# Two blocks of scores share one mask product, and GpSimd lays out q, in an attention kernel that feeds a mixture of experts

## The chip, the core and the metric

The kernel runs on one core of a Trainium2 chip. The metric is the device time of one execution in microseconds. Before the change the median of three runs is 191.55 us (190.66 to 191.68). One execution was recorded by the hardware profiler; all durations of single instructions come from it.

## The reference

Sliding-window causal attention over 8 batches, 8 heads, 576 positions and a head size of 64, followed by a soft mixture of experts with 8 experts of 4 slots each. Cut to what matters:

```python
scores = scale * np.matmul(q, k.transpose(0, 1, 3, 2))
mask = (rel >= 0) & (rel < 64)               # rel = query position - key position
scores = np.where(mask, scores, -1000000000.0)
scores = scores - np.max(scores, axis=-1, keepdims=True)
attn = np.exp(scores)
attn = attn / (np.sum(attn, axis=-1, keepdims=True) + 1e-09)
x = np.matmul(attn, v)                       # then heads side by side: 4608 x 512
logits = x @ phi                             # 512 x 32
d = softmax of logits over the 4608 tokens   # d.T @ x gives the 32 slots
slot_out[e] = np.maximum(slot_input[e] @ w1[e], 0.0) @ w2[e]      # 512 -> 1024 -> 512
out = (softmax of logits over the 32 slots) @ slot_out
```

All inputs and the output are fp32 in HBM; the kernel computes in fp16 with fp32 accumulation, and the loads of GpSimd's queue convert on the way.

## The kernel before

**Units.** Two heads of one batch make a pair: 32 pairs, numbered p, four to a batch. The 576 positions of a pair are nine blocks of 64 queries, and the window makes each block see 128 keys. One group of loads is two pairs, so there are 16 groups of k, of q and of v.

**q and k.** Rows of q and k arrive with 96 partitions and are turned by TensorE (`st_transpose`, twelve products) into the PSUM banks `a_q` and `a_k`. `st_copy_k` copies k to `kTs` in one 128x576 instruction. `st_copy_q` copies q to `qbs` in two instructions of 64 partitions, one per head: `qbs` holds for each block the two heads beside each other, each with zeros in the other head's partitions, so that one product of 128 columns gives both heads' scores. The zeros are written once (`zero_q`).

**Maxima and scores.** The scores are made twice. First with queries in the partitions: `st_max` lays down the window's mask (two products of 512 columns) and adds eight blocks in `a_m`; `st_max_read` (L356) takes the eight maxima into `ms`; the ninth block has a place of its own (`st_max8`, `st_max8_read`, L366). `st_shift` (L369, L370) turns the nine columns of maxima into nine rows of `rts`. Then `st_scores` makes the scores with keys in the partitions (L375) and adds to each block one more product (L378): `lh` carries the mask in its upper 64 rows and, for block i, a row of minus ones that picks row i of `rts`, so mask and maximum are taken off together. ScalarE exponentiates (`st_exp` L384, `st_exp8` L397) and `st_av` (L408) multiplies by v; a column of ones in v gives the sum. `st_norm` (L417, L418) normalises into `x_b`. `fr_transpose` and its copy turn `x_b` for the logits; `fr_logits`, `fr_exp`, `fr_slots` and `fr_acc` keep a running softmax over tokens, once per batch of four pairs.

**Order.** The order of the instructions of every engine is written out by hand (`manual_schedule`). The loop `for n in range(-1, NP - 1)` handles several pairs at once: in iteration n it turns k of pair n+1 and q of pair n, makes the maxima of pair n-1 (they read q and k of n-1), the shift and the scores of pair n-2, and the value products, normalisation and turn of pair n-4. The first four iterations (`early`) have another order. `kv` marks the iterations in which VectorE copies k (L327) instead of ScalarE (L330): n = 2, and then every fourth.

**GpSimd's queue.** `loads(n)` stands at the head of iteration n. It issues a weight where `WSLOTS` has one (one every 3.2 iterations, 12 in all with the last two), for odd n a load of k, for even n `shift_v`, then a load of v and one of q. `shift_v` (L183, L185) moves v by half a chunk between partitions with two copies, and so waits until that v has landed. `loads` and the softmax's `cb_sub` are all that GpSimd does in the loop. A 1 MB weight (fp16) is one load; v, k and q are 288 KB each. v has two buffers, k and q four.

**After the loop** the last pairs are finished in an order of their own, the last weights are loaded in pieces into buffers that have come free (`load_last1`, `load_half`), the running softmax is closed, and the experts are multiplied (`first`, `second`, `second_last`); the half columns 0 to 255 of the experts' output are done before the other half. `give` makes the output in pieces and SyncE's queue writes them (L905).

Of the kernel before, what the change touches and what calls it, by code (L numbers as in the profile page):

```python
# [18 lines left out]
def kernel(  # L19
# [141 lines left out]
    pqk = ctx.enter_context(tc.tile_pool(name="pqk", bufs=1))  # L161
    pvv = ctx.enter_context(tc.tile_pool(name="pvv", bufs=1))
    pw = ctx.enter_context(tc.tile_pool(name="pw", bufs=2))
    pxb = ctx.enter_context(tc.tile_pool(name="pxb", bufs=2))
    pxt = ctx.enter_context(tc.tile_pool(name="pxt", bufs=1))

# [9 lines left out]
    def shift_v(g):  # L176
        b, gq = divmod(g, 2)
        v1, v2 = v1s[b % 2], v2s[b % 2]
        c0, c1 = NVC * gq, NVC * gq + NVC

        w1, w2 = [t[:, :, :].rearrange("p c x -> p (c x)").bitcast(mybir.dt.int32)
                  .rearrange("p (c x) -> p c x", c=NCH)[:, :, 0:Dh // 2] for t in (v1, v2)]
        nc.gpsimd.tensor_copy(out=w2[64:128, c0:c1, :], in_=w1[0:64, c0:c1, :])  # L183
        c0 = max(c0, 1)
        nc.gpsimd.tensor_copy(out=w2[0:64, c0:c1, :], in_=w1[64:128, c0 - 1:c1 - 1, :])  # L185
# [5 lines left out]
    def warm_up(n):  # L191
        for i in range(n):
# [11 lines left out]

    db = const.tile([128, 12], FP16, name="db")
    nc.vector.tensor_scalar(out=db[64:128, 0:NB], in0=ident_h[64:128, 64:64 + NB], scalar1=-1.0, scalar2=None,
                            op0=ALU.mult)
    nc.vector.tensor_scalar(out=db[64:128, 10:11], in0=ident_h[64:128, 64 + NB:65 + NB], scalar1=NEG, scalar2=None,  # L210
                            op0=ALU.mult)
    nc.vector.tensor_copy(out=db[64:128, 11:12], in_=ident_h[64:128, 64 + NB:65 + NB])
    lh = const.tile([128, NB, 128], FP16, name="lh")
    nc.scalar.copy(out=lh[64:128], in_=db[64:128, 0:NB].unsqueeze(2).broadcast_to([64, NB, 128]))

    NK, NQ = 4, 3
    kTs = [pqk.tile([128, 64 + S], FP16, name=f"kT{i}") for i in range(NK)]
# [11 lines left out]

    no_token()  # L230
    round_rows("ks", 0, nc.scalar.copy)
    nc.vector.tensor_copy(out=lh[0:64], in_=wb[:, :].unsqueeze(1).broadcast_to([64, NB, 128]))
# [4 lines left out]
    nc.vector.memset(wm[:, 0, 0:64], NEG)  # L237
    round_rows("ks", 1, nc.vector.tensor_copy)
    NR = 2
    rts = [const.tile([128, 128], FP16, name=f"rt{i}") for i in range(NR)]  # L240

    def make_rt(rt):
        nc.vector.tensor_copy(out=rt[64:128, :], in_=db[64:128, 11:12].broadcast_to([64, 128]))
        nc.vector.tensor_copy(out=rt[0:64, 0:64], in_=ident_h[0:64, 0:64])
        nc.vector.tensor_copy(out=rt[0:64, 64:128], in_=ident_h[0:64, 0:64])


    ms = [const.tile([128, 128], FP16, name=f"m{i}") for i in range(2)]
# [12 lines left out]
    ssf = const.tile([128, 4, 32], FP32, name="ssf")  # L261
    quarter = const.tile([128, 4], FP32, name="quarter")
    emask = const.tile([128, 2], FP32, name="emask")

    def late_constants(n):
        if n == 0:
            nc.vector.memset(ms[0], 0.0)
            zero_q(1)
        elif n == 1:
            nc.vector.tensor_tensor(out=lh[64:128, 0, 0:64], in0=lh[64:128, 0, 0:64],  # L270
                                    in1=db[64:128, 10:11].broadcast_to([64, 64]), op=ALU.add)
            make_rt(rts[0])
            nc.vector.memset(ms[1], 0.0)
            zero_q(2)
        elif n == 2:
            make_rt(rts[1])
        elif n == 3:
            ones_v(0)
        elif n == 4:
            ones_v(1)  # L280
        elif n == 5:
            nc.vector.tensor_copy(out=phi_sb, in_=phi_f)
            nc.vector.memset(quarter, 0.0)
            for d_ in ds:
                nc.vector.memset(d_[:, 192:256], 0.0)
            nc.vector.memset(nmax[1], 1.0e30)
            nc.vector.memset(stat, 0.0)
        elif n == 7:
            for t in range(4):
                nc.vector.tensor_copy(out=ss[32 * t:32 * t + 32],  # L290
                                      in_=ident_h[32 * t:32 * t + 32, 32 * t:32 * t + 32]
                                      .unsqueeze(1).broadcast_to([32, 4, 32]))
                nc.vector.memset(quarter[32 * t:32 * t + 32, t:t + 1], 1.0)
        elif n == 15:
            nc.vector.tensor_copy(out=ssf, in_=ss)
# [26 lines left out]
    def turned(tq):  # L322
        return tq[:, 0:S].rearrange("p (r g) -> p g r", r=RQ)

    def st_copy_k(p, on_vector=False):
# [3 lines left out]
        else:  # L329
            nc.scalar.activation(kTs[p % NK][:, 64:64 + S], turned(a_kh), AF.Copy, scale=QKS)  # L330

    def st_copy_q(p, both=False):
        for hf in range(2):
            h = slice(64 * hf, 64 * hf + 64)
            if hf and both:
                nc.vector.tensor_scalar(out=qbs[p % NQ][h, :, hf, :], in0=turned(a_qh)[h], scalar1=QKS, scalar2=None,  # L336
                                        op0=ALU.mult)
            else:
                nc.scalar.activation(qbs[p % NQ][h, :, hf, :], turned(a_qh)[h], AF.Copy, scale=QKS)  # L339
# [13 lines left out]
                             start=False, stop=True, skip_group_check=True)  # L353

    def st_max_read(p):
        nc.vector.reduce_max(ms[p % 2][:, 64:72].rearrange("p (l c) -> p l c", l=2),  # L356
                             a_m[:, :, :].rearrange("p l (c x) -> p l c x", x=128), axis=AXX)

    m8 = a_v[:, 0, 384:512]

# [2 lines left out]
        nc.tensor.matmul(m8, qblock(p, 8), kwindow(p, 8), start=False, stop=True, skip_group_check=True)  # L363

    def st_max8_read(p, m8=m8):
        nc.vector.reduce_max(ms[p % 2][:, 72:73], m8, axis=AXX)  # L366

    def st_shift(p, t_=a_v[:, 1, 384:512]):
        nc.tensor.matmul(t_, ms[p % 2][:, :], ident_h[:, :], start=True, stop=True, skip_group_check=True)  # L369
        nc.vector.tensor_copy(out=rts[p % NR][64:64 + NB, :], in_=t_[64:64 + NB, :])  # L370

    def st_scores(p, blocks, at):
        rt = rts[p % NR]
        for i in blocks:
            nc.tensor.matmul(at(i), kwindow(p, i), qblock(p, i), start=(i % 4 == 0), stop=False,  # L375
                             skip_group_check=True)
        for i in blocks:
            nc.tensor.matmul(at(i), lh[:, i, :], rt[:, :], start=False, stop=True, skip_group_check=True)  # L378

    def st_score(p):  # L380
        st_scores(p, range(8), lambda i: a_s[:, i // 4, 128 * (i % 4):128 * (i % 4) + 128])
# [111 lines left out]

    def cb_exp(b):
        ec = pw.tile([128, 6, 32], FP16, name="ec", tag="ec") if b < B - 1 else \
            lh[:, 6:8, :].rearrange("p i x -> p (i x)")[:, 0:192].rearrange("p (i s) -> p i s", s=32)
        nc.scalar.activation(ec[:, :, :], lgs.pop(b)[:, :, :], AF.Exp)
        cbs[b] = ec

# [42 lines left out]
    def loads(n):  # L542
        if n in WSLOTS:
            load_w(WSLOTS[n])
        i, odd = divmod(n, 2)
        if odd:
            if 0 <= i < NG - 4:
                load_k(i + 4)
        elif i > 0:
            shift_v(i - 1)  # L550
            if i + 1 < NG:
                load_v(i + 1)
            if i + 3 < NG:
# [97 lines left out]
    def make_ss4():  # L651
        nc.gpsimd.memset(ss4, 0.0)
        for t in range(4):
            r = slice(32 * t, 32 * t + 32)
            nc.gpsimd.tensor_copy(out=ss4[r, t, :], in_=ss[r, :, :].rearrange("p t s -> p (t s)"))
# [34 lines left out]
    for d in range(2):  # L690
        load_half(d)
    st_score8(p - 3)
# [71 lines left out]
    ssf_ = ssf[:, :, :].rearrange("p t s -> p (t s)")  # L764
# [205 lines left out]
```

## Time and profile before

| what | value |
|---|---|
| median of three runs | 191.55 us (190.66 to 191.68) |
| the profiled execution | 190.24 us, span 188.2 us |
| TensorE busy (matmul) | 160.0 us, 85% |
| VectorE busy | 142.9 us, 76% |
| ScalarE busy | 145.0 us, 77% |
| GpSimd busy | 83.0 us, 44% |
| granted TensorE clock | 0.978 of full speed on average, full until the last two slices |
| read from HBM, written | 61.93 MB, 9.44 MB |
| q copies (L339) | 63, 645 ns each |
| k copies on ScalarE (L330), on VectorE (L327) | 24 of 655 ns, 8 of 746 ns |
| shift copy (L370) | 30, 289 ns each |
| v's loads, issue to landing | 13.3 us median, 8.8 to 19.1 |

How to read it: a line such as `L370 DVE CAST rt<-a_v` is the instruction of line 370 on VectorE (DVE) that writes `rt` and reads `a_v`. PE is TensorE's matmul, PEld its weight load, ACT is ScalarE, POOL GpSimd. Square brackets in a timeline give the idle time of the engine before the instruction and what ended it. The DMA row gives the busy share of the 16 DMA engines in forty slices of the span; a share over 1 in a table of stretches means that packets overlap within an engine.

### The profile page before, as it was taken

The numbers are of one execution on the slowest core, as the hardware profiler recorded it, in microseconds if no ns is written. First come the engines' busy times: TensorE is split into PE (matmuls) and PEld (weight loads), VectorE is DVE, ScalarE is ACT, GpSimd is POOL, SyncE is SP. The second block draws the span as 40 slices with busy tenths as digits, with TensorE's granted clock in tenths as the row PEclk, the third lists the DMA queues.
The fourth block names the chain that finished last, engine by engine and source line by source line (L and its number), as shares of the span: only waits on it lengthen the run. The fifth ranks groups of instructions, "written<-read, shape, count | busy, mean of one in ns | idle before, by whom it ended". The sixth has DMA issues, their size and how long they took to land.

```text
span 188.2 us, 7073 instructions
## 1 busy us (share of the span) xinstructions
PE 160.0 (85%) x3039; PEld 120.5 (64%) x3039; DVE 142.9 (76%) x354; ACT 145.0 (77%) x267; POOL 83.0 (44%) x123
## 2 busy tenths in 40 slices
PE   5777999999999999999999999999899899878400
PEld 1466778877777677777777787777785357543100
DVE  6797786897888789788888878897887734689700
ACT  6677879989889899889898898989478455589500
POOL 7955726171682453862953706707653170000000
PEclk9999999999999999999999999999999999999965
DMA  6999999999999999999999999999999999999996
GB/s 160 223 184 185 228 172 226 175 222 180 185 223 180 213 191 185 201 206 181 209 193 191 211 187 190 203 202 192 216 211 216 205 196 193 247 340 392 417 417 264
DMA packets 62302, 41.47 MB, mean 220 GB/s; under 512 B 38848, under 2 KB 58304, under 8 KB 61376
## 3 DMA queue, kind: packets, MB, share of 16 engines
q0 software_dynamic: 56560, 30.35, 116.7%
q1 hardware_dynamic: 5712, 10.68, 16.0%
q8 instruction: 23, 0.38, 0.7%
q14 instruction: 7, 0.06, 0.1%
HBM read 61.93 MB, written 9.44 MB: 379 GB/s over the span
## 4 chain that ended last, share of the span: by engine, by line
PE 45%; DVE 34%; ACT 6%; DMA 5%; issue 4%; DVEq 0%; SPq 0%; ACTq 0%
DVE m L356 10%; PE a_m L349 5%; DVE x_b L418 5%; PE a_m L352 5%; PE a_v L408 4%; PE a_s L375 4%; PE a_s L378 4%; PE a_q L319 3%; DMA out_dram<-w 3%; PE a_k L432 3%; DVE kT L327 3%; DVE rt L370 2%; DVE acc L529 2%; DMA w<-in_q_dram 2%; PE ha L819 2%
## 5 line engine op out<-in xcount | busy, mean ns | idle before, releaser
L339 ACT ACTIVATE qb<-a_q 64x576 f16<-64x576 f16 x63 | 40.6, 645 | 6.1 <-PE a_q L319 4.9
L356 DVE TENSOR_REDUCE m<-a_m 128x8 f16<-128x1024 f32 x32 | 39.1, 1223 | 1.0
L384 ACT ACTIVATE pt<-a_s 128x1024 f16<-128x1024 f32 x32 | 32.8, 1023 | 6.8 <-PE a_s L378 5.6
L183 POOL COPY v<-v 64x576 int32<-64x576 int32 x16 | 10.6, 661 | 41.1 <-DMA v<-in_v_dram 41.0
L418 DVE TENSOR_TENSOR x_b<-a_v,rc 128x640 f16<-128x640 f32 x31 | 25.6, 824 | 1.1
L352 PEld LDWEIGHTS <-qb 128*128 128x128 f16 x256 | 16.9, 98 | 7.6 <-DVE qb L336 0.3
L349 PE MATMUL a_m<-wm,ident_h 128*128 128x512 f16 x64 | 19.3, 384 | 1.4 <-DVE m L356 1.4
L378 PEld LDWEIGHTS <-lh 128*128 128x128 f16 x288 | 18.7, 98 | 2.0 <-issue 1.7
L173 POOL DMA_DIRECT2D v<-in_v_dram x16 | 19.7, 1234 | 0.0
L375 PEld LDWEIGHTS <-kT 128*128 128x128 f16 x288 | 18.6, 98 | 1.6 <-issue 1.4
L436 ACT COPY xt<-a_k 128x576 f16<-128x576 f16 x28 | 17.9, 639 | 2.2 <-PE a_k L432 0.9
L375 PE MATMUL a_s<-qb,kT 128*128 128x128 f16 x256 | 19.5, 219 | 0.0
L378 PE MATMUL a_s<-rt,lh 128*128 128x128 f16 x256 | 19.5, 219 | 0.0
L352 PE MATMUL a_m<-kT,qb 128*128 128x128 f16 x256 | 19.5, 219 | 0.0
L408 PE MATMUL a_v<-v,pt 128*64 128x65 f16 x558 | 15.6, 196 | 2.4 <-DVE m L366 1.1
L79 POOL DMA_DIRECT2D ks<-in_k_dram x15 | 10.5, 697 | 16.0 <-PE a_s L378 3.8
L370 DVE CAST rt<-a_v 9x128 f16<-9x128 f32 x30 | 8.7, 289 | 10.8 <-PE a_v L369 10.5
L408 PEld LDWEIGHTS <-pt 128*64 128x64 f16 x576 | 13.5, 110 | 4.7 <-DVE m L366 1.8
L330 ACT ACTIVATE kT<-a_k 128x576 f16<-128x576 f16 x24 | 15.7, 655 | 0.8 <-PE a_k L319 0.8
L319 PE MATMUL a_q<-ident_h,qs 96*64 96x96 f16 x384 | 14.8, 206 | 1.2 <-DVE a_q L228 1.1
L319 PE MATMUL a_k<-ident_h,ks 96*64 96x96 f16 x384 | 14.4, 212 | 1.0 <-DVE ks L110 0.8
L901 DVE TENSOR_SCALAR w<-cp,rcs 128x256 f32<-128x256 f32 (+1 forms) x24 | 13.4, 610 | 2.3 <-PE cp L896 1.9
(183 smaller groups left out, 327.8 us busy)
## 6 DMA issues: line engine op xcount, KB each, us to landing
w<-in_moe_w_dram POOLq DMA_DIRECT2D x13, 1024.0 KB, 18.0
out_dram<-w SPq DMA_DIRECT2D x8, 768.0 KB, 6.8
v<-in_v_dram POOLq DMA_DIRECT2D x16, 288.0 KB, 13.3
ks<-in_k_dram POOLq DMA_DIRECT2D x15, 288.0 KB, 15.4
qs<-in_q_dram POOLq DMA_DIRECT2D x15, 288.0 KB, 13.5
out_dram<-w SPq DMA_DIRECT2D x3, 384.0 KB, 4.0
w1h<-in_moe_w_dram POOLq DMA_DIRECT2D x4, 256.0 KB, 16.7
w<-in_moe_w_dram POOLq DMA_DIRECT2D x4, 256.0 KB, 15.3
```

Of the source, the lines that this page charges most:

```text
L173: nc.gpsimd.dma_start(out=v1s[b % 2][:, c, 0:Dh], in_=v[b].rearrange("h s d -> (h s) d").rearrange("(c p) d -> p c d", p=128)[:, c, :])
L319: nc.tensor.transpose(tq[64 * hf:64 * hf + 64, RP * r:RP * r + RP], src[0:RP, h + hf, Dh * r:Dh * r + Dh], ident_h[0:RP, 0:RP])
L339: nc.scalar.activation(qbs[p % NQ][h, :, hf, :], turned(a_qh)[h], AF.Copy, scale=QKS)
L349: nc.tensor.matmul(a_m[:, j, :], ident_h[:, :], wm[:, j:j + 4, :].rearrange("p c x -> p (c x)"), start=True, stop=False, skip_group_check= ...
L352: nc.tensor.matmul(a_m[:, i // 4, 128 * (i % 4):128 * (i % 4) + 128], qblock(p, i), kwindow(p, i), start=False, stop=True, skip_group_chec ...
L356: nc.vector.reduce_max(ms[p % 2][:, 64:72].rearrange("p (l c) -> p l c", l=2), a_m[:, :, :].rearrange("p l (c x) -> p l c x", x=128), axis ...
L375: nc.tensor.matmul(at(i), kwindow(p, i), qblock(p, i), start=(i % 4 == 0), stop=False, skip_group_check=True)
L378: nc.tensor.matmul(at(i), lh[:, i, :], rt[:, :], start=False, stop=True, skip_group_check=True)
L384: nc.scalar.activation(st_pt(p)[:, 0:8, :].rearrange("p i x -> p (i x)"), a_s[:, :, :], AF.Exp, scale=XS)
L408: nc.tensor.matmul(a_v[r0:r0 + 64, hf, 65 * (i // 2):65 * (i // 2) + 65], pt[:, i, 64 * hf:64 * hf + 64], rhs, start=True, stop=True, skip ...
L418: nc.vector.tensor_tensor(out=xbs[b][:, :, 128 * hp:128 * hp + 128].rearrange("p c (l d) -> p l c d", l=2), in0=avv[:, :, :, 0:64], in1=rc ...
L436: nc.scalar.copy(out=xts[b][:, hp, :], in_=th[:, 0:S])
```

## The change

- `lh` has five entries instead of nine. An entry now picks a row for each of two neighbouring blocks, and one product of 256 columns takes mask and maxima off both; the ninth block keeps a product of 128 columns. `rts` is 256 wide. The maxima of even blocks lie in columns 64 to 68 of `ms`, those of odd blocks in columns 96 to 99; the shift's copy becomes a multiplication by `kind`, which zeroes the rows of the other kind in each half.
- From pair 4 to pair 30 q leaves PSUM in one 128x576 copy of ScalarE into `qp` (one buffer), and GpSimd copies its two halves from there into `qbs`, as int32. The first four pairs and the last keep `st_copy_q`.
- k is copied by ScalarE in every iteration but n = 2.
- `loads(n + 1)` stands behind the q copies of iteration n (from n = 3). Weights are issued every 3.6 iterations, nine instead of ten before the last two slots, and one more after the loop; the last `shift_v` moves behind it.
- The fp32 copy `ssf` is made by GpSimd after the loop, in `qp`'s buffer, instead of by VectorE in iteration 15.

```diff
+    NJ = NB // 2 + 1
     db = const.tile([128, 12], FP16, name="db")
-    nc.vector.tensor_scalar(out=db[64:128, 0:NB], in0=ident_h[64:128, 64:64 + NB], scalar1=-1.0, scalar2=None,
+    nc.vector.tensor_scalar(out=db[64:128, 0:NJ], in0=ident_h[64:128, 64:64 + NJ], scalar1=-1.0, scalar2=None,
                             op0=ALU.mult)
+    nc.vector.tensor_tensor(out=db[64:128, 0:NJ], in0=db[64:128, 0:NJ], in1=ident_h[64:128, 96:96 + NJ],
+                            op=ALU.subtract)
...
-    lh = const.tile([128, NB, 128], FP16, name="lh")
+    lh = const.tile([128, NJ, 128], FP16, name="lh")
...
+    kind = const.tile([128, 2, 128], FP16, name="kind")
+    def make_kind():
+        for e in range(2):
+            r = slice(64 + 32 * e, 96 + 32 * e)
+            nc.vector.memset(kind[r, e, :], 1.0)
+            nc.vector.memset(kind[r, 1 - e, :], 0.0)
...
+    def st_copy_q_whole(p):
+        qp = pqp.tile([128, S], FP16, name="qp", tag="qp")
+        nc.scalar.activation(qp, turned(a_qh), AF.Copy, scale=QKS)
+        for hf in range(2):
+            h = slice(64 * hf, 64 * hf + 64)
+            nc.gpsimd.tensor_copy(out=qbs[p % NQ][:, :, :, :].rearrange("p i l x -> p (i l x)").bitcast(mybir.dt.int32)
+                                  .rearrange("p (i l x) -> p i l x", i=NB, l=2)[h, :, hf, :],
+                                  in_=qp[h, :].bitcast(mybir.dt.int32).rearrange("p (i x) -> p i x", i=NB))
...
-        nc.vector.reduce_max(ms[p % 2][:, 64:72].rearrange("p (l c) -> p l c", l=2),
-                             a_m[:, :, :].rearrange("p l (c x) -> p l c x", x=128), axis=AXX)
+        m = ms[p % 2][:, 64:128].rearrange("p (e x) -> p e x", e=2)[:, :, 0:4]
+        nc.vector.reduce_max(m.rearrange("p e j -> p j e"),
+                             a_m[:, :, :].rearrange("p l (j e x) -> p (l j) e x", e=2, x=128), axis=AXX)
...
-        nc.vector.tensor_copy(out=rts[p % NR][64:64 + NB, :], in_=t_[64:64 + NB, :])
+        nc.vector.tensor_tensor(out=rts[p % NR][64:100, :].rearrange("p (e x) -> p e x", e=2),
+                                in0=t_[64:100, :].unsqueeze(1).broadcast_to([36, 2, 128]), in1=kind[64:100],
+                                op=ALU.mult)
...
         for i in blocks:
-            nc.tensor.matmul(at(i), lh[:, i, :], rt[:, :], start=False, stop=True, skip_group_check=True)
+            if i == 8:
+                nc.tensor.matmul(at(i), lh[:, 4, :], rt[:, 0:128], start=False, stop=True, skip_group_check=True)
+            elif i % 2 == 0:
+                nc.tensor.matmul(a_s[:, i // 4, 128 * (i % 4):128 * (i % 4) + 256], lh[:, i // 2, :], rt[:, :],
+                                 start=False, stop=True, skip_group_check=True)
...
-    WSLOTS = {16 * i // 5: i for i in range(10)}
-    WSLOTS.update({NP - 2: 10, NP - 1: 11})
+    WSLOTS = {18 * i // 5: i for i in range(9)}
+    WSLOTS.update({NP - 2: 9, NP - 1: 10})
...
     for n in range(-1, NP - 1):
-        loads(n)
+        if n < 4:
+            loads(n)
...
-        kv = n == 2 or n % 4 == 1 and not early
+        kv = n == 2
...
         if live(n) and not early:
-            st_copy_q(n)
+            st_copy_q_whole(n)
+        if n >= 3:
+            loads(n + 1)
...
-    loads(NP - 1)
     m8k = a_k[:, 0:128]
+    ssf = pqp.tile([128, S // 2], FP32, name="ssf", tag="qp")[:, 0:128].rearrange("p (t s) -> p t s", t=4)
+    load_last1()
+    load_last1()
+    load_w(11)
+    shift_v(NG - 1)
     load_last1()
     load_last1()
     load_w(12)
-    shift_v(NG - 1)
-    load_last1()
-    load_last1()
     make_ss4()
+    nc.gpsimd.tensor_copy(out=ssf, in_=ss)
```

More of the change, by code (lines that the diff above doesn't have):

```diff
@@ L163 @@
     pw = ctx.enter_context(tc.tile_pool(name="pw", bufs=2))
+    pqp = ctx.enter_context(tc.tile_pool(name="pqp", bufs=1))
     pxb = ctx.enter_context(tc.tile_pool(name="pxb", bufs=2))
@@ L203 @@
     load_q(3)
+    NJ = NB // 2 + 1
     db = const.tile([128, 12], FP16, name="db")
-    nc.vector.tensor_scalar(out=db[64:128, 0:NB], in0=ident_h[64:128, 64:64 + NB], scalar1=-1.0, scalar2=None,
+    nc.vector.tensor_scalar(out=db[64:128, 0:NJ], in0=ident_h[64:128, 64:64 + NJ], scalar1=-1.0, scalar2=None,
                             op0=ALU.mult)
-    nc.vector.tensor_scalar(out=db[64:128, 10:11], in0=ident_h[64:128, 64 + NB:65 + NB], scalar1=NEG, scalar2=None,
+    nc.vector.tensor_tensor(out=db[64:128, 0:NJ], in0=db[64:128, 0:NJ], in1=ident_h[64:128, 96:96 + NJ],
+                            op=ALU.subtract)
+    nc.vector.tensor_scalar(out=db[64:128, 10:11], in0=ident_h[64:128, 110:111], scalar1=NEG, scalar2=None,
                             op0=ALU.mult)
-    nc.vector.tensor_copy(out=db[64:128, 11:12], in_=ident_h[64:128, 64 + NB:65 + NB])
-    lh = const.tile([128, NB, 128], FP16, name="lh")
-    nc.scalar.copy(out=lh[64:128], in_=db[64:128, 0:NB].unsqueeze(2).broadcast_to([64, NB, 128]))
+    nc.vector.tensor_copy(out=db[64:128, 11:12], in_=ident_h[64:128, 110:111])
+    lh = const.tile([128, NJ, 128], FP16, name="lh")
+    nc.scalar.copy(out=lh[64:128, 0:NJ], in_=db[64:128, 0:NJ].unsqueeze(2).broadcast_to([64, NJ, 128]))
     NK, NQ = 4, 3
@@ L231 @@
     round_rows("ks", 0, nc.scalar.copy)
-    nc.vector.tensor_copy(out=lh[0:64], in_=wb[:, :].unsqueeze(1).broadcast_to([64, NB, 128]))
+    nc.vector.tensor_copy(out=lh[0:64, 0:NJ], in_=wb[:, :].unsqueeze(1).broadcast_to([64, NJ, 128]))
     round_rows("qs", 0, nc.vector.tensor_copy)
@@ L239 @@
     NR = 2
-    rts = [const.tile([128, 128], FP16, name=f"rt{i}") for i in range(NR)]
+    rts = [const.tile([128, 256], FP16, name=f"rt{i}") for i in range(NR)]
     def make_rt(rt):
-        nc.vector.tensor_copy(out=rt[64:128, :], in_=db[64:128, 11:12].broadcast_to([64, 128]))
-        nc.vector.tensor_copy(out=rt[0:64, 0:64], in_=ident_h[0:64, 0:64])
-        nc.vector.tensor_copy(out=rt[0:64, 64:128], in_=ident_h[0:64, 0:64])
+        nc.vector.tensor_copy(out=rt[64:128, 0:128], in_=db[64:128, 11:12].broadcast_to([64, 128]))
+        nc.vector.memset(rt[64:128, 128:256], 0.0)
+        nc.vector.tensor_copy(out=rt[0:64, :].rearrange("p (i x) -> p i x", x=64),
+                              in_=ident_h[0:64, 0:64].unsqueeze(1).broadcast_to([64, 4, 64]))
+    kind = const.tile([128, 2, 128], FP16, name="kind")
[4 more added lines that the diff above has]
+            nc.vector.memset(kind[r, 1 - e, :], 0.0)
     ms = [const.tile([128, 128], FP16, name=f"m{i}") for i in range(2)]
@@ L260 @@
     ss = const.tile([128, 4, 32], FP16, name="ss")
-    ssf = const.tile([128, 4, 32], FP32, name="ssf")
     quarter = const.tile([128, 4], FP32, name="quarter")
@@ L272, in late_constants @@
             make_rt(rts[0])
+            make_kind()
             nc.vector.memset(ms[1], 0.0)
@@ L294, in late_constants @@
         elif n == 15:
-            nc.vector.tensor_copy(out=ssf, in_=ss)
             nc.vector.memset(emask, 0.0)
@@ L365, in st_max8_read @@
     def st_max8_read(p, m8=m8):
-        nc.vector.reduce_max(ms[p % 2][:, 72:73], m8, axis=AXX)
+        nc.vector.reduce_max(ms[p % 2][:, 68:69], m8, axis=AXX)
     def st_shift(p, t_=a_v[:, 1, 384:512]):
         nc.tensor.matmul(t_, ms[p % 2][:, :], ident_h[:, :], start=True, stop=True, skip_group_check=True)
-        nc.vector.tensor_copy(out=rts[p % NR][64:64 + NB, :], in_=t_[64:64 + NB, :])
+        nc.vector.tensor_tensor(out=rts[p % NR][64:100, :].rearrange("p (e x) -> p e x", e=2),
+                                in0=t_[64:100, :].unsqueeze(1).broadcast_to([36, 2, 128]), in1=kind[64:100],
+                                op=ALU.mult)
     def st_scores(p, blocks, at):
@@ L495, in cb_exp @@
         ec = pw.tile([128, 6, 32], FP16, name="ec", tag="ec") if b < B - 1 else \
-            lh[:, 6:8, :].rearrange("p i x -> p (i x)")[:, 0:192].rearrange("p (i s) -> p i s", s=32)
+            lh[:, 3:5, :].rearrange("p i x -> p (i x)")[:, 0:192].rearrange("p (i s) -> p i s", s=32)
         nc.scalar.activation(ec[:, :, :], lgs.pop(b)[:, :, :], AF.Exp)
@@ L763 @@
     nc.vector.tensor_scalar(out=bd, in0=quarter, scalar1=new[:, :], scalar2=None, op0=ALU.mult)
-    ssf_ = ssf[:, :, :].rearrange("p t s -> p (t s)")
+    ssf_ = ssf.rearrange("p t s -> p (t s)")
     mg = a_q[:, 128:136]
```

## The prediction

> **What bounds the kernel now.** The profiled execution took 190.24 us with a span of 188.2 us; the median of the runs is 191.55 us, 1.31 us more. Costs below are made against the profiled execution and the difference is added to the median. About 0.5% (0.96 us) is what a measurement of this kernel can tell from no change.
>
> I began with the page's slices and then took stretches (us, busy time of PE, PEld, DVE, ACT, POOL, clock, DMA share, GB/s).
>
> ```profile
> DMA  6999999999999999999999999999999999999996
> HBM read 61.93 MB, written 9.44 MB: 379 GB/s over the span
> ```
> ```profile
> 36.00:44.00 8.00, 7.58 (x165) 6.45 (x163) 6.74 (x15) 7.37 (x16) 5.02 (x7) 1.00 1.41 208
> 160.00:164.00 4.00, 3.68 (x79) 2.49 (x77) 3.03 (x8) 2.00 (x6) 0.00 (x0) 1.00 1.02 231
> 176.00:186.00 10.00, 0.47 (x2) 0.00 (x0) 1.64 (x3) 0.82 (x2) 0.00 (x0) 0.70 1.02 417
> ```
>
> The reader sees that the DMA engines have no gap from the first slice to the last: about 200 GB/s of fp16 arrives (twice that is read) until the loads end, then up to 417 GB/s goes out. In the packets the last load ends at 163.4 us, just when the last expert products start; the outputs run from 161.4 to 186.8 us. So a faster loop alone can hardly move the end, while a gap in this stream, or outputs that come late, moves it in full.
>
> The waits say how each engine hangs on this:
>
> ```profile
> POOL v L183 <- DMA v<-in_v_dram: 41.0, 14, 5.5
> DVE rt L370 <- PE a_v L369: 10.5, 21, 0.8
> PE a_k L375 <- ACT kT L330: 1.0, 1, 1.0
> ```
>
> Pool stands 41 us waiting for v to land. DVE and PE wait for each other. PE waits for ACT hardly at all. The timeline of an ordinary pair (DVE) shows the loop that paces it:
>
> ```profile
> 28.60 0.29 DVE L370 CAST rt<-a_v 9x128 f16<-9x128 f32 x1 [0.42 <-PE a_v L369]
> 28.92 1.22 DVE L356 TENSOR_REDUCE m<-a_m 128x8 f16<-128x1024 f32 x1
> 30.06 0.28 DVE L366 TENSOR_REDUCE m<-a_v 128x1 f16<-128x128 f32 x1
> 30.91 0.22 DVE L417 RECIPROCAL rc<-a_v 128x10 f32<-128x10 f32 x1 [0.57 <-PE a_v L408]
> 31.17 0.82 DVE L418 TENSOR_TENSOR x_b<-a_v,rc 128x640 f16<-128x640 f32 x1
> 32.41 0.29 DVE L370 CAST rt<-a_v 9x128 f16<-9x128 f32 x1 [0.42 <-PE a_v L369]
> ```
>
> From rt to rt is 3.81 us: rt 0.32, both maxima 1.42, wait for the value products 0.57, reciprocal and normalisation 1.08, wait for the shift 0.42. No ACT step is in it.
>
> **The change, part by part.**
>
> *q and k copies on ACT.* Two 64x576 copies of 0.645 us become one of 128x576, priced by the k copy of that shape at 0.655 us; every fourth pair gets that k copy as well. ACT has 1.29 - 0.655 - 0.655/4 = 0.47 us less per pair. If all of it paced the loop, 28 pairs would give 13 us; the nearest rows are PE's waits for ACT, 1.0 us once. I take zero: the loop above covers it.
>
> *k copies off DVE.* In one pair of four the chain runs through this copy:
>
> ```profile
> 89.92 0.82 DVE x_b L418
> 90.75 0.67 DVE kT L327
> 91.47 0.44 PE a_k L432 x5
> ```
>
> Without it rt waits for the shift, which takes 0.42 us after the normalisation, so DVE wins not 0.67 but about 0.27 us. PE could start its transposes 0.5 us earlier, but its next value products wait for the small maximum on DVE, so that gives no more.
>
> *rt from 9x128 to 36x256.* Through the rows of 128 elements (289 ns) and of 640 elements (824 ns), both from PSUM, an element costs 1.04 ns; 128 more give +0.134 us (0.42 us each). Bounds: no growth, and 0.473 us, the 256-element accumulation of L529. It is in the loop each time. Per four pairs: +0.134 and -0.27 where k leaves, +0.134, about +0.03 where the accumulator waits for PE anyway, +0.134: together +0.16 us, bounds -0.27 and +0.36.
>
> *Masks in one product.* Eight products of 128 columns come 56 ns apart (0.61 us for eight, 0.22 us of it the latency of one), 0.45 us; four of 256 columns, by the 512-column ones at 0.21 to 0.27 us, take 0.43 to 0.54 us. Pricing this at zero rests on a cover: PE then waits for DVE's small maximum before the value products. Without it the cost is -0.02 to +0.1 us a pair. The Trainium skill (TensorE: Matmul & The Clock Gate, section Back-to-back issue gap) gives about 81 ns per 128-column product in a stream with weight loads; by that rule the halved weight loads would save some 0.2 us per pair (an estimate). The trace's 56 ns disagrees.
>
> *The constants.* The narrower lh (ACT 1.15, DVE 0.74 us before), four small memsets and the ssf cast moved to Pool: the first lie before the wait described next, the cast (0.27 us) in a pair where rt waits 0.65 us for PE. Zero.
>
> *Pool puts q beside zeros.* This decides. Pool works in order. Its queue becomes: q copies of pair n, loads(n+1), q copies of pair n+1. For even n+1, loads first waits for v, moves it, then issues v and q:
>
> ```profile
> 38.83 0.66 POOL L183 COPY v<-v 64x576 int32<-64x576 int32 x1 [2.20 <-DMA v<-in_v_dram]
> 39.30 0.65 PEld L352 LDWEIGHTS <-qb 128*128 128x128 f16 x8
> 39.53 0.66 POOL L185 COPY v<-v 64x576 int32<-64x576 int32 x1
> 40.14 1.23 POOL L173 DMA_DIRECT2D v<-in_v_dram  x1
> 41.36 0.69 POOL L79 DMA_DIRECT2D qs<-in_q_dram  x1
> ```
>
> These are loads(8), and L352 at 39.30 is PE taking q of pair 8. Now q waits behind them: Pool is free at 42.05 us. A 64x288 int32 copy lies between half of 0.661 and the whole; through 32x128 (0.287) and 64x576 (0.661) it is 0.42 us, so two end 0.9 us later, at 42.95: PE stalls 3.65 us (3.45 to 4.05 with the bounds). Nothing brings v earlier: it lands where the stream, without gaps, has got to, and the weight slots ahead of it (0 and 3) stay. Pair 6 gives 2.0 us by the same sum, part of the 3.65. Pairs 10 and 16 would give 4.7 and 5.6, but each has one 1 MB weight fewer ahead of its v (slots 6 and 12 become 7 and 14), 4.9 us at some 214 GB/s. Pair 14 gives 3.2, under what is already lost. So 3.65 us, once. ACT's new wait (a single qp buffer, with the logits copy, xt copy and exponential queued behind it) ends with the same copies and starts when PE's does (39.18 against 39.30); it adds nothing. The Trainium skill (GPSIMD Engine Reference, section 3.1) has a one-input body at 1.03 cycles of 1.2 GHz per element; by it, an estimate, each copy takes about 0.25 us plus dispatch and the sum would fall by some 0.3 us; no run here shows that shape.
>
> *Sum.* 3.65 + 0.16 x 23/4 = 4.6 us for the loop's end. Does DMA hide it? Loads now hang on q copies. Near the end, with a weight fewer ahead, v of loads(26) lands near 121.8 instead of 126.7 us; the weight of slot 28 follows the q copies of pair 27, 115.69 + 4.6 + 1.65 = 121.9 us, and needs some 2 us to its first packet (at the start a load of SP took 1.0 and one of Pool 3.5); slot 30 leaves about 1.3 us more of gap. The weight taken from the loop is loaded after it. So loads end about 4 us late too, and the 9.44 MB of outputs need their 23 us after that. Forecast: +4.6 us: span 192.8, profiled execution 194.8, median 196.1 us. With the bounds the loop loses 1.9 to 6.1 us, 193.5 to 197.7 us.
>
> **The rivals.**
>
> *No difference.* Outputs could start some 1.5 us later (0.6 MB of them went out before the loads ended, at about 0.4 MB per us) without a gap. If v landed before Pool got there, or DVE gained what the stall costs, the gapless stream gives the same end, 191.6 us. For it: that stream, and late in the loop Pool meets v on time (93.41 us, no wait). Against: the early pairs. 0.15.
>
> *Faster.* q copies are in time and weight loads do pace PE: four fewer, 98 ns each in the page's rows against 56 ns a product, save 4 x 42 ns = 0.17 us per pair, 4.7 us in 28, and k's 0.27 us seven times 1.9 us. The time gains only what DMA packs better: outputs of 1 KB pieces (3.1 MB at the 335 GB/s of 164 to 168 us against 417) go beside the loads, at most 1.9 us: 189.7 us. It decides once the outputs start before about 159 us. For it: PE is 85% busy. Against: the gapless DMA and 56 ns. The Trainium skill's rule on weight loads, above, points this way. 0.08.
>
> *Much slower.* All bounds fall on their dear end (6.1 us), and the late gap also holds back the last v, which costs the pairs that use it another 1 to 2 us: 199 us. For it: pair 14 is only 0.4 us from stalling again. Against: it needs every cost at its upper end. 0.09.
>
> That part isn't done as said: the first four pairs and the last keep the old q copies. That costs nothing and takes nothing away.
>
> **How the numbers follow.** Forecast 0.68, no difference 0.15, faster 0.08, much slower 0.09. Range 191.2 to 198.8 us: from the no-difference case to near the much slower one. Faster by over 0.5%: 0.08. Within: the no-difference case and 0.01 of the forecast's low end, 0.16. Slower: 0.76.
>
> **What would show it.** Right: PE's L352 waiting some 2 to 4 us for Pool's copies around 31 to 43 us; rt near 0.42 us; POOL still waiting for v; plain pairs of 3.9 to 4.0 us; a DMA share under 0.9 near 120 to 132 us; first output near 165 us. Wrong: no wait of PE for Pool, or a first output near 160 us with the last load at 163 us again.

## The result, and the profile after

The changed kernel takes 197.07 us (median of 4 runs, 196.69 to 197.66), the kernel before on the same chip 191.23 us: a ratio of 1.031 [1.027, 1.035], or 5.8 us more. The profiled execution took 197.66 us with a span of 195.9 us. One run each of e4, e9 and e12 below was over 1.5% slower than the fastest of its kernel and is left out of their medians and ratios.

The same stretches as before (length; busy time of PE, PEld, DVE, ACT, POOL; clock; DMA share; GB/s), with one more where the prediction expected a gap:

```profile
36.00:44.00 8.00, 6.49 (x141) 5.03 (x140) 5.68 (x19) 5.37 (x13) 6.42 (x11) 1.00 1.79 189
118.00:124.00 6.00, 5.44 (x136) 4.47 (x136) 5.12 (x13) 4.56 (x9) 3.32 (x6) 1.00 0.82 60
160.00:164.00 4.00, 3.29 (x77) 2.60 (x70) 2.10 (x5) 2.00 (x5) 1.61 (x4) 1.00 1.45 197
176.00:186.00 10.00, 5.84 (x37) 2.19 (x35) 7.61 (x13) 6.47 (x11) 0.00 (x0) 1.00 1.03 403
```

Between 36 and 44 us PE has lost 1.1 us and GpSimd is busier; between 118 and 124 us only 60 GB/s arrive. In the kernel before that stretch held

```profile
118.00:124.00 6.00, 5.74 (x142) 4.57 (x141) 5.06 (x14) 5.48 (x11) 3.11 (x5) 1.00 1.38 198
```

Loads now run on to 169.6 us (163.4 before) and the first output starts at 167.7 us (161.4). The waits of the changed kernel (engine, line, releaser: us in total, times, longest):

```profile
POOL v L184 <- DMA v<-in_v_dram: 6.2, 5, 2.2
DVE rt L395 <- PE a_v L394: 14.2, 28, 1.6
PEld L376 <- POOL qb L352: 2.3, 3, 1.6
ACT qp L349 <- POOL qb L352: 2.2, 3, 1.4
PE op L885 <- DMA w2h<-in_moe_w_dram: 1.0, 1, 1.0
```

GpSimd's 41 us of waiting for v are 6.2 (it now waits 21.1 us for ACT's copy `qp` instead), PE and ACT wait for GpSimd, and the last expert products wait 1.0 us for a weight. An ordinary pair on DVE:

```profile
30.17 0.43 DVE L395 TENSOR_TENSOR rt<-a_v,kind 36x256 f16<-36x256 f32 x1 [0.42 <-PE a_v L394]
30.63 1.23 DVE L381 TENSOR_REDUCE m<-a_m 128x8 f16<-128x1024 f32 x1
31.77 0.28 DVE L391 TENSOR_REDUCE m<-a_v 128x1 f16<-128x128 f32 x1
32.62 0.22 DVE L448 RECIPROCAL rc<-a_v 128x10 f32<-128x10 f32 x1 [0.57 <-PE a_v L439]
32.87 0.82 DVE L449 TENSOR_TENSOR x_b<-a_v,rc 128x640 f16<-128x640 f32 x1
```

Only rt has grown, 0.29 to 0.43 us. GpSimd around pair 8:

```profile
36.63 0.93 POOL L352 COPY qb<-qp 64x288 int32<-64x288 int32 x2
38.76 0.66 POOL L184 COPY v<-v 64x576 int32<-64x576 int32 x1 [1.21 <-DMA v<-in_v_dram]
39.46 0.67 POOL L186 COPY v<-v 64x576 int32<-64x576 int32 x1
40.07 1.23 POOL L174 DMA_DIRECT2D v<-in_v_dram  x1
41.29 0.69 POOL L79 DMA_DIRECT2D qs<-in_q_dram  x1
42.02 0.91 POOL L352 COPY qb<-qp 64x288 int32<-64x288 int32 x2
```

The q copies of pair 8 stand behind the wait for v, its moves and two loads, and end at 42.93 us. PE's first product with them starts 4.28 us after v's landing.

### The profile page after: what moved, and what is told of

It reads as the page before. It is cut to its first block, busy times and chain, and to the rows that moved or that the text cites. A ratio compares the mean times of both kernels' runs of the same rounds, so it can differ in the third digit from the quotient of the medians.

```text
span 195.9 us, 6845 instructions
## 1 busy us (share of the span) xinstructions
PE 160.9 (82%) x2911; PEld 118.2 (60%) x2911; DVE 144.3 (74%) x351; ACT 130.3 (67%) x247; POOL 105.5 (54%) x178
## 3 DMA queue, kind: packets, MB, share of 16 engines
HBM read 61.93 MB, written 9.44 MB: 364 GB/s over the span
## 4 chain that ended last, share of the span: by engine, by line
DVE 34%; PE 26%; DMA 20%; issue 5%; POOL 4%; ACT 3%; SPq 0%; DVEq 0%; ACTq 0%; POOLq 0%
DVE m L381 15%; DMA w2h<-in_moe_w_dram 9%; DMA w1h<-in_moe_w_dram 6%; PE a_m L373 6%; DVE rt L395 5%; PE a_m L376 5%; PE a_q L333 3%; PE a_v L439 3%; DMA w<-in_k_dram 3%; DVE x_b L449 3%; DVE m L391 3%; DMA out_dram<-w 3%; PE a_v L387 2%; DVE w L937 2%; DVE acc L560 2%
## 5 line engine op out<-in xcount | busy, mean ns | idle before, releaser
L352 POOL COPY qb<-qp 64x288 int32<-64x288 int32 x54 | 22.9, 424 | 23.0 <-ACT qp L349 21.1
L395 DVE TENSOR_TENSOR rt<-a_v,kind 36x256 f16<-36x256 f32 x30 | 12.8, 428 | 14.3 <-PE a_v L394 14.2
L349 ACT ACTIVATE qp<-a_q 128x576 f16<-128x576 f16 x27 | 17.6, 654 | 5.3 <-POOL qb L352 2.2
L376 PE MATMUL a_m<-kT,qb 128*128 128x128 f16 x256 | 20.0, 222 | 1.3 <-POOL qb L352 1.1
L344 ACT ACTIVATE kT<-a_k 128x576 f16<-128x576 f16 x31 | 20.3, 654 | 0.6 <-PE a_k L333 0.6
L373 PE MATMUL a_m<-wm,ident_h 128*128 128x512 f16 x64 | 19.9, 393 | 0.7 <-DVE m L381 0.7
L439 PE MATMUL a_v<-v,pt 128*64 128x65 f16 x558 | 15.0, 196 | 6.3 <-DVE m L391 5.7
L439 PEld LDWEIGHTS <-pt 128*64 128x64 f16 x576 | 14.5, 110 | 9.0 <-issue 8.2
L408 PE MATMUL a_s<-rt,lh 128*128 128x256 f16 x128 | 19.2, 273 | 0.2 <-DVE rt L395 0.2
L939 ACT ACTIVATE w<-cp,rcs 128x256 f32<-128x256 f32 (+1 forms) x24 | 12.5, 585 | 3.4 <-PE cp L932 3.2
```

What stands on the lines that cost most here:

```text
L352: nc.gpsimd.tensor_copy(out=qbs[p % NQ][:, :, :, :].rearrange("p i l x -> p (i l x)").bitcast(mybir.dt.int32) .rearrange("p (i l x) -> p i ...
L373: nc.tensor.matmul(a_m[:, j, :], ident_h[:, :], wm[:, j:j + 4, :].rearrange("p c x -> p (c x)"), start=True, stop=False, skip_group_check= ...
L376: nc.tensor.matmul(a_m[:, i // 4, 128 * (i % 4):128 * (i % 4) + 128], qblock(p, i), kwindow(p, i), start=False, stop=True, skip_group_chec ...
L395: nc.vector.tensor_tensor(out=rts[p % NR][64:100, :].rearrange("p (e x) -> p e x", e=2), in0=t_[64:100, :].unsqueeze(1).broadcast_to([36, ...
L439: nc.tensor.matmul(a_v[r0:r0 + 64, hf, 65 * (i // 2):65 * (i // 2) + 65], pt[:, i, 64 * hf:64 * hf + 64], rhs, start=True, stop=True, skip ...
```

## The experiments

Two theories were set against each other: GpSimd's queue costs the time (the prediction's), or the masks with their wider rt, the list of weights, or k on ACT do. After the first four runs a second question stood beside it: does the end follow the loop or the loads? In the table the loop is the time from the first reduction of `a_m` to the last (127.6 us before); last load and first output are the packets of the two queues. These three come from one profiled execution each. The loop leaves out the start, which differs from execution to execution: the first reduction comes at 9.57 us before and at 10.62 us in e6, whose start is the same code, and between 9.6 and 11.0 us in all.

| kernel | median, us | ratio to before [95%] | loop against before | last load | first output |
|---|---|---|---|---|---|
| before | 191.0 to 191.3 | 1 | 0 | 163.4 | 161.4 |
| changed | 197.07 | 1.031 [1.027, 1.035] | +3.9 | 169.6 | 167.7 |
| e1: q on ACT | 195.01 | 1.023 [1.017, 1.029] | +3.0 | 163.9 | 165.8 |
| e2: v later | 199.00 | 1.042 [1.035, 1.049] | +5.5 | 171.8 | 170.2 |
| e3: old weights | 197.22 | 1.034 [1.028, 1.039] | +6.0 | 166.0 | 168.2 |
| e4: narrow masks | 193.53 | 1.016 [1.008, 1.023] | +0.3 | 165.8 | 164.3 |
| e5: masks alone | 195.97 | 1.026 [1.022, 1.030] | +4.7 | 162.9 | 166.2 |
| e6: k alone | 191.29 | 1.000 [0.998, 1.003] | +0.3 | 163.7 | 162.7 |
| e7: q on Pool alone | 195.91 | 1.024 [1.020, 1.028] | +4.0 | 164.8 | 166.4 |
| e9: one weight less | 190.75 | 0.997 [0.993, 1.000] | -0.4 | 159.7 | 161.7 |
| e10: late weights earlier | 196.90 | 1.026 [1.021, 1.032] | +4.5 | 164.9 | 168.2 |
| e11: v after q | 195.59 | 1.022 [1.017, 1.027] | +3.1 | 168.1 | 166.5 |
| e12: narrow, mended | 191.21 | 1.000 [0.997, 1.003] | -0.1 | 164.2 | 162.5 |

### e1: the Pool part taken out

```diff
-        if n < 4:
-            loads(n)
+        loads(n)
...
-            st_copy_q_whole(n)
-        if n >= 3:
-            loads(n + 1)
+            st_copy_q(n)
...
+    loads(NP - 1)
```

> The changed kernel with the q copies put back on ACT, straight from PSUM, and the loads back at the head of each pair; the two-block masks, the k copies on ACT and the new list of weight slots stay. My theory (q and the loads hang on GpSimd's one queue): GpSimd's wait for v holds nobody again, PE has no wait for GpSimd, the load stream has no gap after 120 us or only one of under 1 us, the last load lands by about 165 us, and the time falls by 4 to 6 us to 191 to 193 us, although the vector write of rt still takes 0.43 us in each pair. Rival 1 (the new weight list by itself opens the late gap, one weight fewer in the loop): the gap and the last load near 169 us stay, 195 to 197 us. Rival 2 (the wider rt and masks cost the time): the loop stays as slow, 195 to 197 us, with no gap named.

195.01 us: less than the changed kernel by 2.1 us going by the medians, 1.5 by the ratios, not by 4 to 6. The loads are healed (last load 163.9 us), and yet the kernel is 4 us slower than before. The page's DMA slices (tenths) show a hole after the loads:

```profile
DMA  6999999999999999999999999999999998499996
```

The loads are done and the outputs are not ready. So the loop, not the stream, holds the end, and the masks cost much more than the prediction's sum gave them when GpSimd's wait isn't there to cover them.

### e2: the move of v behind the odd pair's load of k

```diff
         if odd:
             if 0 <= i < NG - 4:
                 load_k(i + 4)
+            if i > 0:
+                shift_v(i - 1)
         elif i > 0:
-            shift_v(i - 1)
```

> The changed kernel with GpSimd's move of v taken from the even pair's loads to the odd pair's, so that the q copies of the even pair no longer stand behind the wait for v; the loads of v and q of the even pair are issued without that wait. My theory: the stall of PE for GpSimd near 40 us (2.3 us in all) goes, the maximum of pair 8 comes 1 to 2 us earlier than in the changed kernel, the wait for v shows up one pair later, when v has nearly landed (it lands about 3.8 us before that). The start's 1.6 us stays and the loads of k and of weights still follow the q copies, so the late gap stays in part: 194 to 196 us. Rival (the wait for v is only moved by a pair and stalls the next q copies as long): 197 us, with GpSimd's copies late in odd pairs.

199.00 us, slower: the rival's side, but for another reason. GpSimd's timeline:

```profile
36.30 0.68 POOL L79 DMA_DIRECT2D ks<-in_k_dram  x1 [3.33 <-PE a_s L408]
37.02 0.72 POOL L184 COPY v<-v 64x576 int32<-64x576 int32 x1
37.80 0.64 POOL L186 COPY v<-v 64x544 int32<-64x544 int32 x1
38.50 0.89 POOL L352 COPY qb<-qp 64x288 int32<-64x288 int32 x2
```

The wait for v is gone, but the load of k still waits for its buffer (3.3 us, until 36.30; in the changed kernel 2.1 us, until 35.91), and the two moves (1.4 us) now follow it, so the q copies of pair 7 end at 39.39 us (37.56 in the changed kernel) and pair 7 takes 6.9 us in place of 4.5. (Some 0.8 us of that is PE at a granted clock of 0.50 from 39.6 to 43.0 us: from PE's first load of q to the reduction pass 2.3 us here, 1.5 there.) What counts is everything ahead of q in the queue, not the wait for v alone.

### e3: the weight slots of before

```diff
-    WSLOTS = {18 * i // 5: i for i in range(9)}
-    WSLOTS.update({NP - 2: 9, NP - 1: 10})
+    WSLOTS = {16 * i // 5: i for i in range(10)}
+    WSLOTS.update({NP - 2: 10, NP - 1: 11})
```

(The order of the tail's loads is that of before, too.)

> The changed kernel with the weight slots of before (ten in the loop, every 3.2 pairs, the order of before in the tail). My theory: one more weight is queued ahead in the loop, so the late gap shrinks (loads in flight near 120 us), but pairs 10 and 16 get their q copies behind v with one 1 MB weight more ahead of it (4.9 us at some 214 GB/s), so the loop falls behind by 5 to 7 us in place of 4.5: 195 to 198 us, about the same time or a little less. Rival (the weight list by itself opened the gap): no gap near 120 us, last load at 164 to 165 us, 191 to 193 us.

197.22 us, as expected: no gap near 120 us and the last load 3.5 us earlier, but pairs 10 and 16 (5.73 and 4.60 us in place of 4.48 and 4.18) wait for q, the loop loses 2 us more, and the time is the same.

### e4: the masks of before

```diff
-                nc.tensor.matmul(a_s[:, i // 4, 128 * (i % 4):128 * (i % 4) + 256], lh[:, i // 2, :], rt[:, :],
+            nc.tensor.matmul(at(i), lh[:, i, :], rt[:, :], start=False, stop=True, skip_group_check=True)
...
-    rts = [const.tile([128, 256], FP16, name=f"rt{i}") for i in range(NR)]
+    rts = [const.tile([128, 128], FP16, name=f"rt{i}") for i in range(NR)]
```

> The changed kernel with the masks and maxima of before (eight products of 128 columns, rt of 9x128, lh of nine blocks); the q copies on GpSimd, the k copies on ACT and the new weight slots stay. My theory: rt goes from 0.43 to 0.29 us, the start comes 0.5 to 1 us earlier as fewer constants are made, the plain pair takes 3.81 us again; the GpSimd wait at pair 8 grows by what the start gained (v lands when the stream brings it), and the late gap stays nearly as it is: 195.5 to 197 us. Rival (rt and the wide masks cost most): 191 to 194 us.

193.53 us (192.69 to 195.18), less than the changed kernel by 3.5 us going by the medians, 2.9 by the ratios: more than this theory allowed, and the slow end of the rival's band. The masks are the larger part of the 5.8 us. After pair 9 the loop gains 1.7 us on the kernel before, where the changed kernel loses 1.2; that is 0.13 us a pair, rt's growth. PE's first maximum product of pair 8 is 3.22 us late here and 3.47 in the changed kernel: v's landing fixes that moment, whatever stood before it: in the five kernels with this order (the changed one, e3, e4, e7 and e10) v lands between 38.45 and 39.95 us, and the product follows 4.28 to 4.29 us later in each.

### e5: the masks alone

The kernel before with the masks, rt, lh and constants of the change; of the rest only the cast to `ssf` on GpSimd after the loop.

> The kernel before with the two-block masks and maxima alone (36x256 rt, half-width lh, the new constants); q copies on ACT, k copies on DVE every fourth pair, weight slots and loads as before. My theory after the first four runs (the end follows the later of two clocks, the loop's and the loads'): the constants cost 1.0 us at pair 1 and rt costs 0.14 us in each pair without cover, together 4.5 to 5.5 us at the last maximum; the loads keep their pace (last load by 164.5 us), so a hole of some 3 to 4 us opens in the DMA stream ahead of the outputs and the time is 195.5 to 197 us. Rival (the prediction's: the DMA stream alone sets the end and hides a slower loop but for some 1.5 to 2 us): 192 to 194 us.

195.97 us, as the newer theory had it. Pair 1 takes 0.9 us more: its rt starts 0.75 us later (13.34 against 12.59 us) behind the new constants, and takes 0.14 us longer. Then a plain pair takes 3.95 to 3.98 in place of 3.81 to 3.84 us; the loop ends 4.7 us late. Loads end at 162.9 us. In the stretch from 161 to 168 us, first the kernel before, then this one:

```profile
161.00:168.00 7.00, 5.63 (x97) 4.06 (x89) 5.01 (x13) 4.27 (x12) 0.00 (x0) 1.00 1.03 307
```

```profile
161.00:168.00 7.00, 6.35 (x119) 4.86 (x118) 3.89 (x10) 3.95 (x10) 0.00 (x0) 1.00 0.36 91
```

The DMA engines stand idle for two thirds of it. None of the loop's 4.7 us is hidden.

### e6: k on ACT alone

```diff
-        kv = n == 2 or n % 4 == 1 and not early
+        kv = n == 2
```

> The kernel before with all k copies from pair 4 on on ACT, nothing else. Both theories: the seven pairs with a k copy lose 0.27 us each, the last maximum comes about 1.9 us earlier. Theory 1 (the later of two clocks; the loads end where they did): no change beyond 0.5 us, 190.5 to 191.5 us. Rival 1 (the loop alone sets the end): 189 to 189.5 us. Rival 2 (ACT gets so much busier, 145 to about 150 us, that it paces pairs): the loop is slower, 192 us.

191.29 us, no change; but the loop isn't shorter. A pair that loses the k copy takes 3.81 in place of 4.09 us (-0.28), as forecast, and the next 4.14 to 4.25 in place of 3.84 to 3.94 (+0.20 to +0.41). The waits between 35 and 120 us say why:

```profile
PE a_k L375 <- ACT xt L436: 2.1, 5, 0.5
```

ACT, with both q copies and the k copy, is late with `xt`, whose bank the next product needs. The saving exists where q leaves ACT as well: in e4 and e12 the pair after the k copy stays at 3.81 to 3.84 us, but for one of 4.03 to 4.06. It exists beside the wide masks too, with q still on ACT: e1's loop is 1.7 us shorter than e5's, and what sets these two apart in the loop is k on ACT and the list of weights.

### e7: q on GpSimd alone

The kernel before with `st_copy_q_whole` and the loads behind it; masks, k copies and weight slots of before.

> The kernel before with the q copies through one buffer to GpSimd and the loads behind them, nothing else (masks, k copies on DVE and weight slots of before; the cast of ss goes to GpSimd as its tile shares the buffer). Theory (GpSimd's queue): PE waits for GpSimd in pairs 6 to 8, 10 and 16, together 2.5 to 4 us at the last maximum, the loads end 1 to 3 us later; time 193.5 to 195 us. Rival (the weight slots of the change, not the queue, cost the loads' time): loads end at 163 to 164 us and the time stays within 1 us of before.

195.91 us, 1 us above the expected band. Its waits:

```profile
PEld L360 <- POOL qb L336: 4.4, 4, 2.6
```

By pair 9 the loop is 4.5 us behind (pairs 8 and 9 took 6.03 and 5.04 us) and then wins back 0.6. Of pair 9, 1.2 us are PE itself: after its 2.1 us of waiting for GpSimd the granted clock is 0.51 from 45.2 to 48.6 us, and eight of its products take 1.06 us in place of 0.61. By the medians this part alone is as dear as the masks alone (4.7 us each), while both with k on ACT and the new list of weights cost 5.8. How much of the difference is cover is shown for the masks: alone they lengthen the loop by 4.7 us (e5), on top of the rest by 3.6 (changed against e4). The rest of it is also k on ACT and the list of weights.

### e8 and e9: one weight less

> The kernel before with one 1 MB weight of the first product not loaded (expert 3 reads expert 2's tile instead), so 1 MB of fp16 less arrives, some 4.9 us of the stream; no other edit. It asks whether the loop or the loads set the end of the kernel before. Theory 1 (two clocks that end together): the last load comes 4 to 5 us earlier, the outputs start at most 0.5 us earlier, as the loop is unchanged, and the time falls by 0 to 0.7 us: 190.3 to 191.2 us. Rival (the DMA stream alone sets the end): 186.5 to 189 us.

196.05 us, and no answer to the question: the weights' tiles are also the output's buffers (`obs`), and two experts now shared one, so that the writers of the output waited for the transfer of an earlier piece:

```profile
ACT w L905 <- DMA out_dram<-w: 10.5, 2, 5.5
```

e9 keeps the tile as a buffer and leaves out only the load:

```diff
-        w1_t[e] = [w1[:, kk, :] for kk in range(NKK)]
+        w1_t[e] = [(w1_t[2, 0] if e == 3 else w1)[:, kk, :] for kk in range(NKK)]
...
-        if n in WSLOTS:
+        if n in WSLOTS and WSLOTS[n] != 3:
```

> The kernel before with the first-product weight of expert 3 not loaded (its products read expert 2's tile; its own tile stays as an output buffer, which the earlier kernel with one weight less had shared between two experts and so stalled its own outputs). 1 MB of fp16 less, some 4.9 us of the stream. Theory (two clocks that end together, and the loop's is not changed): the last load comes 4 to 5 us earlier, a hole of 1 to 2 us opens in the DMA stream ahead of the outputs, the first output starts at most 0.5 us earlier and the time falls by 0 to 1 us: 190.3 to 191.3 us. Rival (the DMA stream alone sets the end): 186.5 to 189 us.

190.75 us: the last load comes 3.7 us earlier and the time falls by 0.3 us going by the medians, 0.7 by the ratio. Stretches from 155 us:

```profile
155.00:161.00 6.00, 5.35 (x107) 3.91 (x103) 3.23 (x9) 3.48 (x11) 0.51 (x1) 1.00 0.46 63
161.00:168.00 7.00, 5.62 (x101) 4.25 (x101) 5.19 (x13) 4.45 (x12) 0.00 (x0) 1.00 0.86 283
```

The stream runs dry before the outputs, and they start at 161.7 us all the same. The loads are not what holds the kernel before.

### e10: the late weights earlier

```diff
-    WSLOTS = {18 * i // 5: i for i in range(9)}
-    WSLOTS.update({NP - 2: 9, NP - 1: 10})
+    WSLOTS = {18 * i // 5: i for i in range(7)}
+    WSLOTS.update({24: 7, 26: 8, 28: 9, 30: 10})
```

> The changed kernel with its last weights in the loop issued earlier (slots 24, 26, 28 and 30 in place of 25, 28, 30 and 31; the tail is the same). It asks what the late gap in the loads costs beside the slower loop. Theory (the end follows the loop, which is 4.5 us behind; the gap adds only what PE waits for the last expert products, 1.2 us): no gap at 120 to 122 us, last load at 164 to 166 us, and the time falls by 0.8 to 1.8 us to 195.3 to 196.3 us. Rival (the gap is the main cost): 191.5 to 193.5 us. Rival (the late v now lands behind a weight more and stalls GpSimd): 197 us or more.

196.90 us; the difference of 0.2 lies within the spread, short of the 0.8 to 1.8 us expected. The late gap is closed

```profile
118.00:124.00 6.00, 5.45 (x121) 4.10 (x120) 5.16 (x12) 4.58 (x10) 2.51 (x5) 1.00 1.32 193
```

and the last load is 4.7 us earlier, but this execution's loop is 0.6 us longer (pairs 6 to 8 took 0.7 us more), and in place of PE's wait for the weight its earlier expert products take 0.7 us longer, since the granted clock is one half where they start:

```profile
154.50:157.90 3.40, 3.34 (x25) 1.03 (x26) 1.29 (x5) 0.78 (x2) 1.25 (x2) 0.50 1.46 197
```

This trace cannot price the gap. Others can: from the first of the last expert products to the first output product pass 2.64 us in the changed kernel and in e4, where PE waits for the weight, and 1.40 to 1.53 us in all others. So the gap holds the first output product up by 1.2 us.

### e11: the move of v right behind q

```diff
         if odd:
+            if i > 0:
+                shift_v(i - 1)
             if 0 <= i < NG - 4:
                 load_k(i + 4)
         elif i > 0:
-            shift_v(i - 1)
```

> The changed kernel with GpSimd's move of v put right behind the q copies of the even pair, ahead of the odd pair's load of k (the earlier try put it behind that load, where it held up the q copies of the odd pair). Theory (GpSimd's order decides): the stalls at pairs 7 and 8 shrink from 1.5 us to under 0.5 us and the last maximum comes about 1 us earlier than in the changed kernel; the late gap shrinks by as much: 195 to 196.3 us. Rival (the move and its wait only stall other pairs): pair 7 or 9 takes 5 us or more, 196.5 to 199 us.

195.59 us, 1.5 us less, as expected:

```profile
39.81 0.91 POOL L352 COPY qb<-qp 64x288 int32<-64x288 int32 x2
40.78 0.66 POOL L184 COPY v<-v 64x576 int32<-64x576 int32 x1
41.48 0.67 POOL L186 COPY v<-v 64x576 int32<-64x576 int32 x1
```

The q copies of pair 8 end at 40.72 us, 2.2 us earlier; pair 8 takes 3.95 in place of 5.15 us. This execution's start is 0.6 us earlier, and its loop 0.8 us shorter. The gap at 120 us is still there (87 GB/s from 118 to 124 us), the masks' cost too.

### e12: what is left when the masks go and the queue is mended

e4 with e11's order and e10's slots.

> The changed kernel with the masks of before, the move of v behind the even pair's q copies and the last weights of the loop earlier (slots 24, 26, 28, 30): what is left of the change is q on GpSimd and k on ACT. Theory: no stall over 0.5 us at pairs 6 to 8, seven pairs 0.27 us shorter, so the last maximum comes 1 to 1.9 us earlier than before; the loads end near 163.5 us as before and set the start of the last products, so the time is that of before within 1 us: 190.3 to 191.8 us. Rival 1 (the loop alone sets the end): 189.3 to 190.2 us. Rival 2 (GpSimd's moves still hold up q): 192 to 194 us.

191.21 us, no difference from before. Pairs 6 to 8 still lose about 1.1 us (pair 7 took 5.48 us), more than the stalls of under 0.5 us that were expected; the pairs without a k copy on DVE win it back. The last maximum comes when it does in e4 (138.2 and 138.3 us), and the first output 1.8 us earlier: PE waits 1.1 us for the last weights in e4 and not here (last load 165.8 and 164.2 us). So with a loop no longer than that of before, loads that come late do hold back the end. The ratios (1.016 and 1.000) are 3 us apart, more than these two executions explain.

## Why the prediction was right, and where not

The forecast was 196.1 us; 197.07 were measured, inside the range and on the side forecast. Between the two profiled executions the first output moved by 6.3 us: 0.6 by the start, 3.9 by the loop, 0.4 on the way from the last maximum to the last expert products, 1.2 by their wait for a weight, and 0.1 behind it. The forecast's 4.6 us stand beside the 4.5 by which the last maximum moved, but 0.6 of these are luck: they are the start of this execution, in which the granted clock was 0.50 from 8.4 to 11.8 us. By its steps:

**GpSimd's order.** Right in place and size: q copies of pair 8 from 42.05 to 42.95 us were forecast and came from 42.02 to 42.93; PE takes up pair 8 3.47 us later than before (3.65). Five kernels show the mechanism: PE takes up pair 8 4.28 to 4.29 us after v's landing in each (4.18 by the forecast's sum). But 3.65 us is how late the loop is there, not what the queue alone adds. Without it (e1) 1.5 to 2.1 us of the 5.8 come back, since what it covers then shows.

**Constants at zero.** The cover that was named held: pair 8 starts 0.25 us apart with and without them (3.47, 3.22). Where the cover is gone they cost 0.75 us (e5). No price without cover was given, and it should have been.

**rt and k.** rt took 0.428 us (0.42) and 0.13 us a pair; -0.27 us for a pair without the k copy is right in e4 and e12. From pair 9 on the changed kernel lost 1.2 us, by the sum 0.9. ACT's relief was put at zero ("the loop above covers it"); e6 shows what it is good for: beside the narrow masks k on ACT gives nothing without it.

**Masks at zero.** A plain pair grew by 0.14 us, all of it rt's; on PE the four wide products of an ordinary pair took the 0.45 us of the eight narrow ones. By the 81 ns a product of the Trainium skill (TensorE: Matmul & The Clock Gate, Back-to-back issue gap) half the weight loads would have saved some 0.2 us a pair, an estimate; no run shows a saving.

**The late gap.** It came where it was put (the weight of slot 28 was issued at 121.4 us, forecast 121.9), but the loads ended 6.2 us late, not 4: the mis-sized term. The sum then gave it no time of its own beside the loop. PE waits 1.0 us for a weight, and the first output product comes 1.2 us later by it (e4 and the changed kernel against all others), which is part of why the first output came at 167.7 us and not near 165.

**What bounds the kernel.** This reading failed in what it says of a gap. "A faster loop alone can hardly move the end, while a gap in this stream, or outputs that come late, moves it in full": a gapless stream only shows that it is busy. With 3.7 us less of loads (e9) the stream has a gap and the end moves 0.3 us the other way; with the loop 4.7 us longer and the loads on time (e5) it moves 4.7. That late outputs move the end in full was right; that a faster loop would not is untested. The "no difference" rival lived on that reading and gives 1.5 us of slack that isn't there. The forecast survived because it took the outputs' start from the loop. The Trainium skill (Perfetto Trace Analysis, Identifying the Most-Contended Engine) says that occupancy misleads for DMA, since there are 16 engines. Here too a busy share did not tell what sets the end (e9, e5), though the DMA row is a mean over the 16.

**What stays open.** No run had a shorter loop than before by more than 0.4 us, so whether the loads would hold back a faster one is not shown; the first outputs of e4 and e12 speak for it. The medians differ from the loop's differences by up to 2.5 us (e2, e4): the wait for the last weights (1.2 us) is one part, the starts and the clock of single executions are others, and the 0.4 us ahead of the last expert products in the changed kernel were not taken apart. The profiled execution of the changed kernel also took 0.6 us more than its median, and that of before (190.24 us) 1.0 us less than its own.

## What to carry to other kernels

A DMA row of nines does not say that the stream sets the end: leave one load out, or slow the loop, and see which moves it. Before work is moved to a queue that also issues loads, list everything that stands ahead of it there, waits, moves and issues, and price the covered edits once with and once without their cover: the masks lengthened the loop by 4.7 us alone and by 3.6 beside the rest. What a part is worth depends on the others: k on ScalarE gave nothing by itself, 1.7 us of the loop beside the wide masks and the new list of weights. And look at the granted clock of a single execution before its stalls are put down to the edit.

## What was not expected of the hardware

The outputs (9.44 MB) take 25.1 to 27.3 us from their first packet to their last in all kernels but e8: 25.1 to 26.7 in the seven with loads still running beside their start, 25.3 to 27.3 in the six where the loads had ended 1.7 to 3.3 us earlier. No gain from a stream without loads is seen. A copy of 64x288 int32 on GpSimd takes 424 ns against 661 for twice the width, so about 190 ns are fixed. The Trainium skill (GPSIMD Engine Reference, section 3.1) gives some 0.25 us for its body, an estimate; with those 190 ns the two agree.

In six of the fourteen profiled executions the granted TensorE clock fell to 0.50 for 3.41 us at a time while PE still had work, besides the fall at the very end: at 8.4 us in the changed kernel, at 8.9, 39.6 and 155.7 in e2, 45.2 in e7, 167.1 and 177.3 (twice as long) in e8, 154.5 in e10 and 152.0 in e11. In the 3.41 us ahead of each, PE had been busy for 2.44 us or less, in e7 for 1.3. Such stretches also occur without a fall (2.1 us busy of the 3.41 that end at 43.8 us in the changed kernel), so a stall of PE may or may not cost a second time.
